# Laying the value stage's stationary operands 192 bytes, not 64, from its moving ones

## The chip, the cores and the metric

One core of a Trainium2 chip runs the whole kernel. The metric is the device time in microseconds, as the median of several executions. A profiled execution of the kernel before supplies the rows below; its engines are TensorE (PE for matmuls, PEld for its weight loads), VectorE (DVE), ScalarE (ACT), GpSimd (POOL) and SyncE (SP).

## The reference, cut to what matters

Eight sequences of 576 tokens with 8 heads of 64 go through attention inside chunks of 64 tokens, and its output through a channel mix. All is float32.

```python
scores = scale * q_c @ k_c^T                  # within each chunk of 64 tokens
attn = softmax(scores);  x = attn @ v_c       # x: (8, 576, 512)
x_prev = x moved down by one token
xk = mu_k * x + (1 - mu_k) * x_prev
xr = mu_r * x + (1 - mu_r) * x_prev
k = maximum(xk @ w_k, 0)                      # 512 -> 1024, "key stage"
v = (k * k) @ w_v                             # 1024 -> 512, "value stage"
out = sigmoid(xr @ w_r) * v                   # "receptance stage"
```

## The kernel before, in words

The 4608 tokens are cut into 18 groups of 256. For each group TensorE does, in an order written out by hand (the table `START` for groups 0 and 1 and the loading of the weights, the table `GROUP` for every later group): scores and softmax transposes of the next group, the key stage K (line 636), the receptance stage R (line 689) and the value stage (line 720 for groups 0 to 3, line 910 for groups 4 to 17). The order of every engine's instructions is fixed by these tables.

Each operand of K, R and the value stage is split into a high and a low part in a reduced 32-bit format, and a product takes three matmuls (high by high, high by low, low by high; `PASSES`).

- K: the stationary operand is a 128 by 128 block of the weight `wk`, the moving one 256 tokens of the mixed input `xk`. 18 groups of 96 matmuls.
- R: stationary is a block of the mixed input `xr`, moving are 512 columns of `wr`. 18 groups of 24 matmuls.
- Value stage: stationary is a block of the key stage's results (`kk`, or `ks`, sums of blocks of them), moving are 256 columns of a weight quarter (`b`). Groups 0 to 3 take 96 matmuls each; groups 4 to 17 use seven products of 12 matmuls instead of eight, 84 each.

Every matmul has its own weight load (PEld), which TensorE runs while the matmul before it streams its moving operand. So two reads of on-chip memory (SBUF) go on together: the moving operand of one matmul and the stationary operand of the next.

Where a tile lies in SBUF follows from the order in which `pool(...)` is called on lines 110 to 123: pools are placed one behind the other, and every buffer of a pool has the size of its largest tile. The first pool starts at 128 modulo 256, behind a few constants. Nearly all tiles are multiples of 256 bytes per partition, except, ahead of the stages' operands, three small tiles, each in a pool of its own: `mu2` (64 bytes, pool `par`), the row maxima `m` (64 bytes, pool `par_m`) and the row sums `z` (32 bytes and padding to 64, pool `par_z`). These three shift everything behind them by 64 bytes modulo 256. Bytes of the start addresses, modulo 256, in the built program:

| tiles | pool | before | after |
|---|---|---|---|
| `wr`, `xr` (R: moving, stationary) | rp | 128, 128 | 128, 128 |
| `kk`, `ks` (value stage: stationary), `rr`, weight staging | mx | 128 | 0 |
| `wk` (K: stationary), `b` quarters (value stage: moving) | wts, tmp | 192 | 192 |
| other value weights `b1` | mo | 192 | 192 |
| `xk` (K: moving) | kp | 0 | 0 |
| `mu2` / `m` / `z` | par / par_m / par_z | 128 / 192 / 0 | 192 / 128 / 0 |
| `qT`, `kT`, `p`, `v`, rings | ld, att | 64 | 64 |

Blocks inside these tiles start at multiples of 512 bytes (of 1024 for the weights), so the table holds for every block. "Moving minus stationary", modulo 256, is 64 in K before and after, 0 in R before and after, and in the value stage 64 before and 192 after.

Two short uses of TensorE in the loading stage also matter below: the first three token tiles are mixed by matmuls with diagonal matrices (line 580; 128 columns, plain float32, each instruction shown as two matmul records), stationary `diag` at 192, moving `x`, whose first buffer starts at 64 and whose second starts at 128 modulo 256.

Of the kernel before, what the change touches and what calls it, by code (L numbers as in the profile page):

```python
# [81 lines left out]
def tile_chunk_attention_channel_mix(  # L82
# [24 lines left out]
    def pool(name, bufs=1):  # L107
        return ctx.enter_context(tc.tile_pool(name=name, bufs=bufs))

    const = pool("const")  # L110
    rp = pool("rp")
    mx = pool("mx")
    par = pool("par")
    wts = pool("wts")
    tmp = pool("tmp", 2)
    par_m = pool("par_m")
    kp = pool("kp")
    par_z = pool("par_z")
    ld = pool("ld")
    att = pool("att", 2)  # L120
# [1191 lines left out]
```

## Time and profile before

| | us |
|---|---|
| median of 3 runs | 594.36 |
| the runs | 592.47 to 594.52 |
| the profiled execution | 592.36 |
| its span, first to last instruction | 590.6 |
| TensorE busy in it | 580.4 |
| VectorE busy | 459.2 |
| ScalarE busy | 354.4 |

A matmul's row shows its own latency (about 280 ns for 256 columns), but matmuls overlap: the next starts long before the one before it ends. What a stage costs is therefore the pitch, the time from one matmul's start to the next one's. In a chain or a timeline, a piece or the distance between two starts divided by the number of matmuls between them is the pitch.

### The profile page before, as it was taken

How to read it: one execution, taken by the hardware profiler on the slowest of the kernel's cores; microseconds unless marked ns; L12 is line 12 of the kernel's file. 1: busy time of each engine (PE TensorE's matmuls, PEld its weight loads, DVE VectorE, ACT ScalarE, POOL GpSimd, SP SyncE). 2: the span in 40 equal slices, each digit the busy share in tenths (PEclk: the TensorE clock that was granted, in tenths of full speed). 3: DMA queues.
4: the chain of work that ended last, by engine and by line, in shares of the span. 5: the costliest groups of instructions: out<-in, count | busy, mean ns of one | idle time of the engine just before them, and what ended most of it. 6: DMA issues, size and time to landing. Idle time of an engine off the chain costs nothing.

```text
span 590.6 us, 15313 instructions
## 1 busy us (share of the span) xinstructions
PE 580.4 (98%) x6497; PEld 549.0 (93%) x6497; DVE 459.2 (78%) x763; ACT 354.4 (60%) x530; POOL 0.7 (0%) x6
## 2 busy tenths in 40 slices
PE   8899999999999999999999999999999999999997
PEld 7779999999899999999999999999999999999997
DVE  2799898659698878887877696978797878876734
ACT  4898964535648483838292929292928383747461
POOL 0000000000000000000000000000000000000000
PEclk9999999999999999999999999999999999999999
DMA  9997422432434343434212434343434243010000
GB/s 283 219 319 172 102 52 74 95 76 51 75 76 74 76 72 80 72 84 71 60 23 64 69 87 66 82 71 85 65 86 72 75 66 82 9 50 25 2 37 37
DMA packets 183988, 49.25 MB, mean 83 GB/s; under 512 B 169576, under 2 KB 175728, under 8 KB 183920
## 3 DMA queue, kind: packets, MB, share of 16 engines
q1 hardware_dynamic: 183904, 48.27, 36.3%
q8 instruction: 51, 0.84, 0.6%
q14 instruction: 17, 0.14, 0.1%
q10 hardware_dynamic: 16, 0.00, 0.0%
HBM read 38.80 MB, written 9.44 MB: 82 GB/s over the span
## 4 chain that ended last, share of the span: by engine, by line
PE 90%; DVE 5%; DMA 2%; ACT 1%; SPq 1%; issue 0%; DVEq 0%; ACTq 0%
PE pk L636 33%; PE pr L689 17%; PE vx L910 13%; PE vyz L910 10%; PE pv L720 7%; PE xps L1092 3%; PE s L1018 3%; DMA wr_st<-in_moe_w_r 2%; PE pt L1074 2%; PE mxk L580 1%; PE mxr L580 1%; DVE bs L747 1%; SPq L186 1%; PE xps L494 0%; PE s L410 0%; DVE bs L766 0%
## 5 line engine op out<-in xcount | busy, mean ns | idle before, releaser
L636 PE MATMUL pk<-xkhi,wk 128*128 128x256 f32 x1152 | 208.2, 281 | 0.0
L636 PEld LDWEIGHTS pk<-xkhi,wk 128*128 128x128 f32 x1152 | 177.2, 187 | 1.2
L636 PE MATMUL pk<-xklo,wk 128*128 128x256 f32 x576 | 160.7, 279 | 0.0
L656 ACT ACTIVATE rr<-pk 128x512 f32<-128x512 f32 x56 | 33.0, 589 | 126.7 <-PE pk L636 126.6
L636 PEld LDWEIGHTS pk<-xklo,wk 128*128 128x128 f32 x576 | 108.3, 188 | 0.1
L689 PE MATMUL pr<-wr,xrhi 128*128 128x512 f32 x288 | 92.3, 401 | 0.0
L910 PE MATMUL vyz<-b,kk 128*128 128x256 f32 x504 | 66.1, 279 | 0.0
L910 PE MATMUL vx<-b,ks 128*128 128x256 f32 x504 | 66.1, 279 | 0.0
L910 PEld LDWEIGHTS vx<-b,ks 128*128 128x128 f32 x504 | 62.3, 188 | 0.0
L910 PEld LDWEIGHTS vyz<-b,kk 128*128 128x128 f32 x504 | 62.3, 188 | 0.0
L689 PEld LDWEIGHTS pr<-wr,xrhi 128*128 128x128 f32 x288 | 51.5, 188 | 10.4
L689 PE MATMUL pr<-wr,xrlo 128*128 128x512 f32 x144 | 56.4, 392 | 0.0
L720 PE MATMUL pv<-b,kk 128*128 128x256 f32 x384 | 46.4, 280 | 0.0
L720 PEld LDWEIGHTS pv<-b,kk 128*128 128x128 f32 x384 | 45.8, 188 | 0.2
L747 DVE TENSOR_TENSOR kk<-rr,kk 128x1024 fp32r<-128x1024 f32 x28 | 33.1, 1222 | 10.4 <-ACT kk L894 10.3
L663 ACT ACTIVATE rr<-rr 128x512 f32<-128x512 f32 x56 | 35.4, 633 | 1.8
L939 ACT ACTIVATE u<-vx 128x256 f32<-128x256 f32 x28 | 10.8, 385 | 42.1 <-PE vx L910 42.1
L689 PEld LDWEIGHTS pr<-wr,xrlo 128*128 128x128 f32 x144 | 27.0, 188 | 5.9
L856 DVE TENSOR_TENSOR ss<-rr 128x512 f32<-128x512 f32 x14 | 9.7, 693 | 27.3 <-ACT rr L663 27.3
L1154 DVE SCALAR_TENSOR_TENSOR mk<-d,mu,x 128x256 f32<-128x256 f32 (+3 forms) x80 | 27.7, 414 | 0.4
L1154 DVE SCALAR_TENSOR_TENSOR mr<-d,mu,x 128x256 f32<-128x256 f32 (+3 forms) x80 | 27.5, 412 | 0.0
L1047 DVE TENSOR_REDUCE z<-p 128x16 f32<-128x1024 f32 x15 | 18.2, 1214 | 11.3 <-ACT p L1043 11.3
(130 smaller groups left out, 885.8 us busy)
## 6 DMA issues: line engine op xcount, KB each, us to landing
v<-in_v SPq DMA_DIRECT2D x144, 64.0 KB, 2.4
out<-sg SPq DMA_DIRECT2D x36, 256.0 KB, 2.4
q_ring<-in_q SPq DMA_DIRECT2D x192, 36.0 KB, 2.0
k_ring<-in_k SPq DMA_DIRECT2D x192, 36.0 KB, 2.0
wk_st<-in_moe_w_k SPq DMA_DIRECT2D x4, 1024.0 KB, 12.0
wv_st<-in_moe_w_v SPq DMA_DIRECT2D x4, 1024.0 KB, 7.7
wr_st<-in_moe_w_r SPq DMA_DIRECT2D x2, 1024.0 KB, 10.3
q_ring<-in_q SPq DMA_DIRECT2D x2, 512.0 KB, 6.8
```

Of the source, the lines that this page charges most:

```text
L580: nc.tensor.matmul(m[:, cb, s : s + w], diag[nm, n][:, cb], x[:, cb, c0 : c0 + w], start=(n == 0), stop=(n == 1),)
L636: nc.tensor.matmul(pk[:, e, :], wk[a][:, cb, f * P : (f + 1) * P], xk[b][:, cb, :], start=(n == 0), stop=(n == 3 * NB - 1),)
L656: nc.scalar.activation(r, T[f"pk{g}{fp}"], AF.Relu)
L663: nc.scalar.activation(r, r, AF.Square)
L689: nc.tensor.matmul(pr, xr[a][:, cb, tl * TT : (tl + 1) * TT], wr[b][:, cb, :], start=(n == 0), stop=(n == 3 * NB - 1),)
L720: nc.tensor.matmul(T[f"pv{g}{tl}"][:, cols[c]], kk[a][:, f, tok[tl]], quarter(f // HF, c)[:, b, f % HF, :], start=(f == 0 and n == 0 and c ...
L747: nc.vector.tensor_tensor(to, x, y, ALU.subtract)
L910: nc.tensor.matmul(to, a[i][:, f, :], weight(w, j, f), start=first and f == 0 and n == 0, stop=f == HF - 1 and n == 2, skip_group_check=True,)
L1018: nc.tensor.matmul(T[f"s{g}"][halves[e], j, tl, hp, :], qT[halves[j], hp, cols], kT[halves[j], hp, cols], start=True, stop=True,)
L1047: nc.vector.tensor_reduce(out=T[f"z{g}"], in_=p(), axis=AX.X, op=ALU.add)
L1092: nc.tensor.matmul(T[f"xps{g}"][halves[c], 2 * j + a, tl * TT + e * CH : tl * TT + (e + 1) * CH], T[f"v{2 * g + tl}"][halves[j], hp, e, :] ...
L1154: nc.vector.scalar_tensor_tensor(out=to[:, cb, s : s + w], in0=T[f"d{g}"][:, cb, s : s + w], scalar=mu[:, cb : cb + 1], in1=T[f"xg{g}"][:, ...
```

## The change

Three pools change places; no instruction is added, removed or moved on any engine, and every tile keeps its size.

```diff
     const = pool("const")
     rp = pool("rp")
-    mx = pool("mx")
-    par = pool("par")
+    par_m = pool("par_m")
     wts = pool("wts")
     tmp = pool("tmp", 2)
-    par_m = pool("par_m")
+    par = pool("par")
     kp = pool("kp")
+    mx = pool("mx")
     par_z = pool("par_z")
```

The pool `mx`, which holds the key stage's results, is laid behind `kp`, which holds the mixed key input. `par` and `par_m`, both of 64 bytes, swap, so that the weights stay at 192 and the key input at 0.

## Rows read from the trace of the kernel before

**Rows 1.** The page: span, and busy time of each engine with its share.
```profile
span 590.6 us, 15313 instructions
PE 580.4 (98%) x6497; PEld 549.0 (93%) x6497; DVE 459.2 (78%) x763; ACT 354.4 (60%) x530; POOL 0.7 (0%) x6
```

**Rows 2.** The page: the chain that ended last, shares of the span by engine.
```profile
PE 90%; DVE 5%; DMA 2%; ACT 1%; SPq 1%; issue 0%; DVEq 0%; ACTq 0%
```

**Rows 3.** Waits of TensorE's matmuls, the longest three (us in total, times, longest).
```profile
PE s L410 <- DVE p L430: 1.5, 1, 1.5
PE mxk L580 <- DVE x L515: 1.4, 1, 1.4
PE s L410 <- ACT pT L143: 1.3, 1, 1.3
```

**Rows 4.** One group's period by stretch: busy us (x), clock, DMA share, GB/s.
```profile
199.18:229.33 30.15, 30.15 (x346) 28.61 (x340) 24.71 (x44) 17.90 (x27) 0.00 (x0) 1.00 0.38 76
```

**Rows 5.** Groups of instructions by line and shape: the value stage's matmuls.
```profile
L910 PE MATMUL vyz<-b,kk 128*128 128x256 f32 x504 | 66.1, 279 | 0.0
L910 PE MATMUL vx<-b,ks 128*128 128x256 f32 x504 | 66.1, 279 | 0.0
L720 PE MATMUL pv<-b,kk 128*128 128x256 f32 x384 | 46.4, 280 | 0.0
L910 PE MATMUL vx<-b,kk 128*128 128x256 f32 x168 | 22.1, 280 | 0.0
```

**Rows 6.** Timeline of TensorE, value stage of group 4: start, us, what.
```profile
188.10 1.58 PE L910 MATMUL vx<-b,kk 128*128 128x256 f32 x12
189.52 1.57 PE L910 MATMUL vyz<-b,kk 128*128 128x256 f32 x12
...
196.58 1.57 PE L910 MATMUL vx<-b,ks 128*128 128x256 f32 x12
```

**Rows 7.** The chain in order of time: K of group 1 (start, us).
```profile
67.71 8.48 PE pk L636 x72
```

**Rows 8.** Timeline of TensorE: K of group 0, pieces of one and two matmuls.
```profile
54.06 0.28 PE L636 MATMUL pk<-xklo,wk 128*128 128x256 f32 x1
...
54.40 0.28 PE L636 MATMUL pk<-xklo,wk 128*128 128x256 f32 x1
...
55.76 0.28 PE L636 MATMUL pk<-xklo,wk 128*128 128x256 f32 x1
...
62.11 0.61 PE L689 MATMUL pr<-wr,xrhi 128*128 128x512 f32 x2
```

**Rows 9.** The chain in order of time: R of group 1, behind that K.
```profile
62.27 5.44 PE pr L689 x24
```

**Rows 10.** Timeline of TensorE: R of the last group, behind a K at its usual pitch.
```profile
571.14 0.63 PE L689 MATMUL pr<-wr,xrhi 128*128 128x512 f32 x2
571.61 0.40 PE L689 MATMUL pr<-wr,xrlo 128*128 128x512 f32 x1
...
572.53 0.62 PE L689 MATMUL pr<-wr,xrhi 128*128 128x512 f32 x2
...
573.91 0.61 PE L689 MATMUL pr<-wr,xrhi 128*128 128x512 f32 x2
...
576.63 0.51 PE L910 MATMUL vx<-b,kk 128*128 128x256 f32 x3
```

**Rows 11.** Timeline of TensorE: mixing by diagonal matrices, token tiles 0 and 2.
```profile
26.14 2.05 PE L580 MATMUL mxk<-x,diag_k 128*128 128x128 f32 x16
51.23 2.05 PE L580 MATMUL mxk<-x,diag_k 128*128 128x128 f32 x16
```

**Rows 12.** Timeline of TensorE: first two matmuls of K in group 5, behind the scores.
```profile
199.18 0.38 PE L636 MATMUL pk<-xkhi,wk 128*128 128x256 f32 x1
199.40 0.28 PE L636 MATMUL pk<-xklo,wk 128*128 128x256 f32 x1
```

**Rows 13.** Groups of instructions: subtraction in the value stage's operands, VectorE.
```profile
L747 DVE TENSOR_TENSOR kk<-rr,kk 128x1024 fp32r<-128x1024 f32 x28 | 33.1, 1222 | 10.4 <-ACT kk L894 10.3
L672 DVE TENSOR_TENSOR kk<-relu,kk 128x512 fp32r<-128x512 f32 x16 | 10.8, 686 | 9.5 <-ACT kk L143 9.4
```

## The prediction

> **What bounds the kernel now.** Read the page's first and fourth part together. TensorE is busy for 580.4 of 590.6 us [rows 1] and carries 90% of the chain that ended last [rows 2]. The view of waits shows that its matmuls hardly wait: the three longest waits are 1.5, 1.4 and 1.3 us, once each, all in the loading stage [rows 3]. Then read one period by stretch: in the 30.15 us of a group TensorE is busy throughout, VectorE for 24.71 and ScalarE for 17.90, at a granted clock of 1.00, the 2.4 GHz level [rows 4]. So the time is the sum of TensorE's pitches, and a nanosecond on the pitch of a stage is paid once per matmul, with nothing to hide it; in the other direction a gain is kept, since VectorE has 5.4 us of room in each period and ScalarE 12.
>
> The value stage has 504 + 504 + 384 + 168 = 1560 matmuls [rows 5]. Their pitch: from 188.10 to 196.58 us there are six blocks of 12, so 8.48 us for 72, 117.8 ns [rows 6]. 1560 of these are 183.8 us, 31% of the span. One nanosecond more or less is 1.56 us.
>
> K has the same pitch, 8.48 us for 72 matmuls or 117.8 ns [rows 7], and the same 64 bytes between its operands. 256 columns at 2.4 GHz last 106.7 ns, so each matmul of both stages pays 11.1 ns beyond its columns. Not all of this is fixed. One stretch of K in group 0 runs faster with the same tiles: from 54.40 to 55.76 us it issues 12 matmuls, 113.3 ns each, and from 54.06 to 62.11 there are 71 in 8.05 us, still 113.4 [rows 8]. R behind it runs at 5.44 us for 24 or 226.7 ns [rows 9], exactly twice 113.3 for twice the columns. I call this the smooth pace. Behind a K at its usual pitch, R starts off it: its first six matmuls take 571.14 to 572.53 us, 231.7 ns each, the first two 0.47 us or 235 each; later twelve, from 573.91 to 576.63, are at 226.7 again [rows 10]. So R, with 0 bytes between its operands, falls back to the smooth pace by itself, and K and the value stage, at 64, mostly do not and pay 4.5 ns a matmul. The trace fits a collision of two reads (a moving operand and the next stationary one) that depends on when the two start, and perhaps on the distance of their addresses.
>
> **The change part by part.** No instruction moves, so every count, wait and queue stays. What is new are addresses.
>
> K, R, scores and transposes: the distance between their operands stays 64, 0 and so on. Cost 0. The smooth stretch of K may be lost or another one won: 71 matmuls by 4.5 ns, 0.3 us either way.
>
> The loading stage: weights staged in `mx` are converted elsewhere in memory, same instructions. Cost 0; TensorE waits there for a few us in all [rows 3], and a DMA is indifferent as far as any row tells.
>
> ScalarE and VectorE on `kk`, `rr`, `ks`: a subtraction of 1024 columns takes 1222 ns with both inputs in `mx`, one of 512 takes 686 ns with one input in `mx` and one 64 bytes further, in another pool [rows 13]. Per column that is 1.19 and 1.34 ns, the same once a fixed part of some 150 ns is taken off both. So distance does not show on VectorE; cost 0, and 5.4 us of room in a period hides what might come. If that cover were gone, 1 us in each of 14 periods would be 14 us.
>
> The value stage: the distance goes from 64 to 192, and its pitch is the whole question. No row shows three-pass matmuls of 256 columns at 192, so I bound it. From below by the smooth pace: 113.3 - 117.8 = -4.5 ns, by 1560, -7.0 us. From above by what R pays where it is off the smooth pace: 235 - 226.7 = 8.3 ns in one weight load's worth of stream; added to 113.3 this is 121.6, +3.8 ns, +5.9 us; the rows are rounded to 10 ns, so that the two could have been 240, which gives 126.6, +8.8 ns, +13.7 us. Further off lies a weight load that isn't hidden at all: behind the scores K's first matmul has a pitch of 220 ns [rows 12], which would be +102 ns and +159 us; I exclude it as nothing changes in what is issued ahead, and keep it out of the range. R's mean over six, 231.7 or 5.0 over the smooth pace, would give 118.3, as good as now.
>
> I take 121 ns, near R's dearest rows: +3.2 ns by 1560 is +5.0 us. The profiled execution goes from 592.36 to 597.4. The median of the runs lies 2.0 us above it (594.36), so the forecast is 599.4, in round terms 599. Why the dear side: at 64 the moving operand lies one 64-byte step ahead of the stationary one and runs away from it, since it covers 1024 bytes while the weight load covers 512; at 192 it lies one step behind and must pass it early, in a stream that has no columns in hand yet. K's observed stretch at 113.3 shows that at 64 passing can be free. This is an argument, not a row.
>
> The Trainium skill speaks against any change here. "SBUF — State Buffer", section "Who interferes with whom", gives TensorE two independent read ports, one for the moving operand and one for weight loads, and says that it waits for no one; "TensorE: Matmul & The Clock Gate", section "Back-to-back issue gap", puts the warm gap at columns over 2.4 plus 2.5 ns. By these pages the value stage would be at 109.2 ns at any distance and the change would cost nothing, 594.4; the trace has 117.8 there and 113.3 at best, so the figure does not hold here, while that addresses don't matter remains possible and is the first rival.
>
> **The rivals.** First, no change: the pitch does not care for the distance. For it: plain float32 mixing takes 2.05 us for 16 matmuls when `x` starts 128 bytes from `diag` modulo 256, and 2.05 again when it starts 192 from it [rows 11]; and K has two paces at one and the same distance [rows 7, 8], so timing alone can explain them. Also 192 is 64 on the other side, and a collision might be symmetric. Against it: those mixing matmuls pass 128 columns in about 112 ns, half the rate of the value stage, where a read that is late has time. Time: 594.4, the runs' own 592.5 to 594.5.
>
> Second, faster: at 192 the value stage falls into the smooth pace, as R does at 0 after six matmuls. For it: the pace exists at the same width, and the value stage always follows R, which by then is in it [rows 10]. Against it: K entered from a smooth R in group 1 at 67.71 us and did not stay smooth [rows 7, 9]. Price: -7.0 us, 587.4; with half of its matmuls smooth -3.5, 590.9.
>
> Third, the change does nothing of what it says because a matmul that needs the distance is fed from other tiles: excluded for all but the `b1` weights by the address table, and these lie at 192 as well. So it is given no chance.
>
> The forecast is itself the slower side. It decides from about 119.7 ns on (+1.9 ns, +3 us, the bound of 0.5%).
>
> **How the numbers follow.** Forecast, slower: 0.45. No change: 0.25. Faster: 0.30. A difference under 0.5% (3 us) cannot be told from none here, as three runs alone spread over 2 us. Within the slower case 597.5 to 605.5 is its own range, the top between 121.6 and 126.6 ns. The whole range goes from the smooth pace on a quick run, 587.4 less 1.4, 586, to 605.5. Both signs are real, so the range takes in all three cases, and only a slower pace than any nearby row is left out.
>
> **What would show it.** In the changed kernel's timeline, blocks of 12 value matmuls start every 1.41 us now; 1.45 would show the forecast, 1.36 the smooth pace, 1.41 no change. K must stay at 2.83 us per 24 and R at 2.72 to 2.77 per 12; if K moves too, the distance is not the cause. The engines' order and TensorE's waits should be as before. If the value pitch stands and the time moves, I am wrong on the loading stage or VectorE; if the pitch falls to 113.3, I am wrong on which side of the stationary operand is the better one.

## The result, and the profile after

The changed kernel took 588.29 us, median of 6 runs (586.07 to 588.54), against 593.48 for the kernel before, median of 6 on the same chip (592.42 to 594.52). The ratio is 0.9916 with a 95% interval of 0.99 to 0.9932: faster by 0.84%, some 5 us. The forecast was 599.0, slower. The profiled execution took 586.07 us against 592.36, 6.29 us less, and its span went from 590.6 to 584.3. The times of either kernel fall into two clusters some 2 us apart (before, three runs at 592.42 to 592.59 and three at 594.36 to 594.52; after, one at 586.07 with a mean granted clock of 1.000 and five at 588.22 to 588.54 with 0.997), so that the gain is some 6 us when like is put against like and 5 by the medians, which mix them; single times further down carry the same scatter.

The page, first and fourth part, of the kernel after (span; busy time, share and instructions of each engine; chain by engine):

```profile
span 584.3 us, 15313 instructions
PE 573.4 (98%) x6497; PEld 542.2 (93%) x6497; DVE 459.3 (79%) x763; ACT 354.2 (61%) x530; POOL 0.7 (0%) x6
...
PE 92%; DVE 5%; ACT 1%; DMA 1%; issue 0%; DVEq 0%; ACTq 0%
```

The counts are those of [rows 1], and VectorE and ScalarE are busy as long as before to within 0.2 us. TensorE alone is busy for 7.0 us less. Its longest three waits are the three of [rows 3], the same to the digit, so none of them went.

Groups of instructions by line and shape answer to [rows 5], but tell nothing of the pitch (the second number behind the bar is one matmul's latency); the subtraction of [rows 13] takes 1222 ns as before:

```profile
L910 PE MATMUL vyz<-b,kk 128*128 128x256 f32 x504 | 66.1, 281 | 0.0
L910 PE MATMUL vx<-b,ks 128*128 128x256 f32 x504 | 66.0, 281 | 0.0
L720 PE MATMUL pv<-b,kk 128*128 128x256 f32 x384 | 45.6, 279 | 0.0
```

The pitch is read from starts. The timeline of TensorE in the value stage of group 4 (start, us, what), against [rows 6]: blocks of 12 start 1.41 us apart, and six of them take 186.63 to 195.11, 8.48 us, 117.8 ns a matmul, just as before. In the last group they start 1.36 us apart from the second block on, 113.3 ns:

```profile
186.63 1.57 PE L910 MATMUL vx<-b,kk 128*128 128x256 f32 x12
188.04 1.58 PE L910 MATMUL vyz<-b,kk 128*128 128x256 f32 x12
...
195.11 1.58 PE L910 MATMUL vx<-b,ks 128*128 128x256 f32 x12
...
570.65 1.54 PE L910 MATMUL vx<-b,kk 128*128 128x256 f32 x12
572.03 1.52 PE L910 MATMUL vyz<-b,kk 128*128 128x256 f32 x12
573.39 1.52 PE L910 MATMUL vx<-b,ks 128*128 128x256 f32 x12
574.75 1.52 PE L910 MATMUL vyz<-b,kk 128*128 128x256 f32 x12
```

What did move is K, whose operands lie as far apart as they did. In the chain in order of time, the 96 matmuls of K are one piece per group. Two groups of the kernel before, then the same two after, with the stages that follow:

```profile
259.56 11.50 PE pk L636 x96
...
289.71 11.50 PE pk L636 x96
```

```profile
257.67 11.08 PE pk L636 x96
268.75 0.87 PE pt L1074 x8
269.62 2.75 PE pr L689 x12
272.38 1.09 PE xps L1092 x64
273.47 2.96 PE pr L689 x12
276.43 1.42 PE vx L910 x12
277.84 1.41 PE vyz L910 x12
...
287.41 11.08 PE pk L636 x96
```

0.42 us in each of 13 groups is 5.5 us. One period by stretch is 29.70 us where [rows 4] had 30.15, at the same granted clock of 1.00, 2.4 GHz:

```profile
227.50:257.20 29.70, 29.70 (x351) 28.15 (x345) 24.46 (x40) 17.84 (x26) 0.00 (x0) 1.00 0.39 77
```

Summed from the start times of all matmuls of a stage, within each group:

| Stage | before, us | after, us | groups at the smooth pace, after |
|---|---|---|---|
| K (distance 64 in both) | 202.60 | 197.18 | 3, 4, 6 to 16; group 0 in part, as before |
| value stage (64, then 192) | 181.61 | 180.53 | 0, 1, 17 |
| R (distance 0 in both) | 94.28 | 94.26 | |

K gave 5.4 us, the value stage 1.1, together 6.5 of a span shorter by 6.3. So the question was no longer what a distance of 192 costs, but why K ran faster at a distance that hadn't changed.

**Where in the beat K starts.** The paces point at it. 113.3 ns is 17 times 6.67 ns and R's 226.7 ns is 34 times 6.67 (16 cycles of 2.4 GHz). In the run of the kernel before, all settled stretches of R start at the same remainder modulo 6.67 ns, over 500 us, with a drift of 0.7 ns (up to 1.1 in the other runs). I call that R's beat, and give the start of another matmul as its lag in ns behind it. This is worked out from starts that the trace keeps in whole ns, so it is good to about 0.3 ns:

```
first matmul of K (the pitches from it on)     lag      pace
before, groups 2 to 16   222 117 118 117 118   5.3-6.3  117.8
after, groups 3, 4, 6-16 222 113 113 114 113   1.0-2.0  113.3
after, group 2           222 117 118 117 118   5.7      117.8
after, group 5           222 117 119 117 118   0.7      117.8
```

And the changed distance can move that start: it alters the few irregular pitches with which the value stage ahead of the scores begins. From the last matmul of R in group 11, ten pitches are 227 118 118 120 118 117 119 117 118 118 = 1290 ns before and 233 122 120 117 118 118 117 119 117 118 = 1299 after. 9 ns are one beat and 2.3 ns; K's lag moved from 5.8 on the mean to 1.6, forward by 2.5 modulo 6.67. That is a reading of two traces. The groups that missed fit it as well: group 2 of the kernel after starts where K was off the pace before, at 5.7. Two theories were put against each other: ENTRY (the instant at which K starts chooses its pace; the addresses matter only through it) and ADDRESS (the new places of the tiles make K faster by themselves).

### The profile page after: what moved, and what is told of

Same layout as the page of the kernel before. It is cut to its first block, busy times and chain, and to the rows that moved or that the text cites. A ratio compares the mean times of both kernels' runs of the same rounds, so it can differ in the third digit from the quotient of the medians.

```text
span 584.3 us, 15313 instructions
## 1 busy us (share of the span) xinstructions
PE 573.4 (98%) x6497; PEld 542.2 (93%) x6497; DVE 459.3 (79%) x763; ACT 354.2 (61%) x530; POOL 0.7 (0%) x6
## 4 chain that ended last, share of the span: by engine, by line
PE 92%; DVE 5%; ACT 1%; DMA 1%; issue 0%; DVEq 0%; ACTq 0%
PE pk L636 32%; PE pr L689 17%; PE vx L910 13%; PE vyz L910 10%; PE pv L720 7%; PE xps L1092 3%; PE s L1018 3%; PE pt L1074 2%; PE trq L367 1%; PE trk L367 1%; DMA q_ring<-in_q 1%; PE mxk L580 1%; PE s L410 1%; PE mxr L580 1%; DVE bs L747 1%; PE warm L1221 1%
## 5 line engine op out<-in xcount | busy, mean ns | idle before, releaser
L636 PE MATMUL pk<-xkhi,wk 128*128 128x256 f32 x1152 | 202.7, 278 | 0.0
L636 PEld LDWEIGHTS pk<-xkhi,wk 128*128 128x128 f32 x1152 | 175.4, 188 | 1.2
L747 DVE TENSOR_TENSOR kk<-rr,kk 128x1024 fp32r<-128x1024 f32 x28 | 33.1, 1222 | 10.4 <-ACT kk L894 10.3
L747 DVE TENSOR_TENSOR ks<-ss,ks 128x512 fp32r<-128x512 f32 x42 | 26.5, 686 | 0.0
```

The costliest lines, as they stand in the source:

```text
L636: nc.tensor.matmul(pk[:, e, :], wk[a][:, cb, f * P : (f + 1) * P], xk[b][:, cb, :], start=(n == 0), stop=(n == 3 * NB - 1),)
L747: nc.vector.tensor_tensor(to, x, y, ALU.subtract)
```

## The experiments

**K shifted, nothing moved.** The addresses are those of the kernel before. From group 2 on one more plain float32 matmul of 64 to 67 columns (64 in the diff below) stands right ahead of K's first one, writing where K then starts afresh:

```diff
+            if g >= 2 and fp == 0:
+                nc.tensor.matmul(
+                    pk[:, 0, :64], f32(wk[0][:, 0, :P]), f32(xk[0][:, 0, :64]), start=True, stop=True
+                )
```

> Addresses as before the change. Ahead of K's first matmul in groups 2 to 17 stands one extra plain float32 matmul of 64 columns into K's own accumulator, which K then overwrites. Its four versions (64, 65, 66, 67 columns) differ by one column, estimated at 1.7 ns from the 112 ns that a 128-column record of this kind takes (two records a matmul). Theory ENTRY: K's pace (113.3 or 117.8 ns) is set by the instant at which K is entered, on a beat of about 6.67 ns, and the change moved that instant; then of the four versions at least one has K at 113.3 ns in 10 or more of groups 2 to 16, and at least one has it at 117.8 in 10 or more, though no tile has moved. Theory ADDRESS: K runs at 113.3 because the results kk lie elsewhere (their writes by ScalarE and VectorE no longer meet K's reads); then K stays at 117.8 in groups 2 to 16 of all four versions. The extra matmul itself costs 0.1 to 0.25 us a group, 1.6 to 4 us in all, in every version.

> As e1_shift64 with 65 columns. ENTRY: K's pace in groups 2 to 16 differs from that in at least one of the other three versions by 4.5 ns a matmul, 0.42 us a group. ADDRESS: 117.8 ns here as in the others.

> As e1_shift64 with 66 columns. ENTRY: K's pace in groups 2 to 16 differs from that in at least one of the other three versions by 4.5 ns a matmul, 0.42 us a group. ADDRESS: 117.8 ns here as in the others.

> As e1_shift64 with 67 columns. ENTRY: K's pace in groups 2 to 16 differs from that in at least one of the other three versions by 4.5 ns a matmul, 0.42 us a group. ADDRESS: 117.8 ns here as in the others.

Measured, one run each, against 592.46: 596.55, 598.09, 595.91 and 595.84 us. K was at 117.8 in groups 2 to 17 of all four, so ENTRY's expectation was missed. The chain of the one with 64 columns:

```profile
261.75 0.36 PE pk L632 x2
262.12 11.37 PE pk L640 x96
```

But the edit doesn't only shift. K's first matmul no longer follows 64-column scores, and its pitch fell from 221 to 201 to 205 ns. Nor did the four lengths spread K's start: its lag was 2.8 to 3.8 ns in all four. Its second matmul came at 0.3 to 1.3 with 64 columns and at 4.5 to 5.5 with the other three; in the smooth groups of the changed kernel it comes at 3.2 on the mean. So none of the four hit that place, and the experiment tells neither theory from the other. In the run with 64 columns the value stage of group 17 went at 113.3 ns, with the old distance of 64: the smooth pace there doesn't need 192.

**The scores shifted instead.** The extra matmul now stands ahead of the scores, so K is still entered from the scores and only comes later, by one column (of a matmul shown as two records) from kernel to kernel. Addresses as before; the diff has 58 columns:

```diff
+            nc.tensor.matmul(T[f"s{g}"][:, 0, 0, 0, :58], ident, ident[:, :58], start=True, stop=True)
```

> Addresses as before the change. One extra plain float32 matmul of 57 columns (its result is overwritten) stands ahead of the scores of each group from group 3 on, behind the value stage and so one stage ahead of K, and K itself is entered as before, from the scores. Its four versions have 57, 58, 59 and 60 columns, so that K is entered at instants some 1.7 ns apart (estimated from 112 ns for a 128-column record, two records). Theory ENTRY, sharpened by the first four runs: the instant of K's first matmul, counted modulo 6.667 ns from the beat on which R settles in the same run, was 5.3 to 6.3 ns before the change (K at 117.8) and 1.0 to 2.0 behind it (K at 113.3; 117.8 where it was 0.7 or 5.7). So K is at 113.3 ns in every group whose entry falls at 1.0 to 2.0 and at 117.8 where it falls at 5.3 to 6.3, and of the four versions at least one has 113.3 in most of groups 4 to 16. Theory ADDRESS: 117.8 in groups 3 to 16 of all four. The extra matmul costs 0.1 to 0.3 us a group; a K at 113.3 gives back 0.42 us.

> As e2_delay57 with 58 columns: ENTRY expects K's entry 1.7 ns later on the beat than there, and K's pace by the phase it comes to; ADDRESS expects 117.8.

> As e2_delay57 with 59 columns: ENTRY expects K's entry 3.3 ns later on the beat than there, and K's pace by the phase it comes to; ADDRESS expects 117.8.

> As e2_delay57 with 60 columns: ENTRY expects K's entry 5.0 ns later on the beat than there, and K's pace by the phase it comes to; ADDRESS expects 117.8.

Measured, one run each, against 594.33: 596.28, 589.88, 596.38 and 596.60 us. The lags of K's first matmul, and its pace in groups 2 to 16:

```
columns   lag (mean)     K       time, us
57        0.3-1.3 (0.8)  117.8   596.28
58        1.3-2.2 (1.7)  113.3   589.88
59        2.0-3.0        117.8   596.38
60        3.0-3.7        117.8   596.60
```

Three chains over the same stretch, of 57, 58 and 59 columns; a group's K is 11.50 and 11.51 us in the outer ones and 11.08 between them:

```profile
262.17 11.50 PE pk L636 x96
...
292.47 11.50 PE pk L636 x96
```

```profile
259.79 11.08 PE pk L636 x96
270.87 0.87 PE pt L1075 x8
...
289.69 11.08 PE pk L636 x96
```

```profile
261.80 11.51 PE pk L636 x96
...
292.14 11.51 PE pk L636 x96
```

One column more, and the kernel gains 6.4 us; one more, and it is lost. No tile was moved. ADDRESS falls as the explanation of K: the gain is to be had without the change, and groups 2 and 5 of the changed kernel lack it with the tiles at their new places. The place that K must hit is some 1 ns wide, out of 6.67; group 5 of the changed kernel, with its lag of 0.7, misses it as the kernel with 57 columns does. A column moved the entry by 0.8 ns, half of what I expected.

**Other distances.** Only the order of the pools differs, so that the operands of the value stage (v) and of K lie at a given distance; no instruction moves. One product of seven, the fifth block of 12 in groups 4 to 17, takes the weights `b1` from another pool and stays at 64 in all four. As an example the one with both at 0 (`par` and `par_m` leave their places for ones behind `kp`; the others are of the same kind):

```diff
     rp = pool("rp")
     mx = pool("mx")
-    par = pool("par")
     wts = pool("wts")
     tmp = pool("tmp", 2)
-    par_m = pool("par_m")
     kp = pool("kp")
+    par = pool("par")
+    par_m = pool("par_m")
     par_z = pool("par_z")
```

> Only the order of the pools differs from the kernel before: value operands 0 bytes apart (64 in the products with the weights b1), key operands still 64. Theory ENTRY: distances have no price of their own, a stage runs at 113.3 or 117.8 ns by the instant at which it is entered; so the value stage's groups are each at one of the two, and K's groups too, in whatever mix the new instants give (total 586 to 594.5 us). Theory SELF-SETTLING: R settles on its smooth pace from any start because its operands are 0 bytes apart; then the value stage at 0 does so too, 113.3 ns in nearly all groups but for its first six matmuls of each and the b1 products, 6 us less than before at K's pace of before (587 to 589). Theory DISTANCE (the forecast's): 0 is another price for the value stage, over 117.8 or under 113.3.

> Value operands 128 bytes apart (64 in the products with b1 becomes 64 as moving b1 stays at 192 and ks at 128), key operands 64. ENTRY: each group's stage at 113.3 or 117.8, total 586 to 594.5 us. SELF-SETTLING says nothing here. DISTANCE: a third pace for the value stage.

> Value and key operands both 0 bytes apart. ENTRY: 113.3 or 117.8 in each group's stage by its instant of entry, total between 579 and 594.5. SELF-SETTLING: both stages at 113.3 in nearly all groups, 12 to 14 us less than before (579 to 582). DISTANCE: other paces.

> Key operands 192 bytes apart, value operands 64 as before. ENTRY: the value stage is entered from R as before and stays at 117.8, K is at 113.3 or 117.8 by its instant; total 587 to 594.5. DISTANCE: K shows a pace of its own at 192.

Measured, one run each, against 594.48, with the sums from the start times:

```
value  K     time, us   value stage                 K
0      64    591.61     184.57 us, 120.0            196.66 us, 113.3 in groups 2-16
128    64    595.97     183.79, 120.0, later 118.6  202.60, 117.8
0      0     600.52     184.57, 120.0               206.60 us, 120.0 everywhere
64     192   586.25     181.62, 117.8               196.21 us, 113.3 in groups 2-17, 0 in part
```

In the first three kernels the block with `b1` runs at 117.8 ns behind blocks at 120.0. Chains over the same stretch, of value 0 and K 0, of value 128 and K 64 (in both the block of 1.42 or 1.41 us is the one with `b1`), then of value 64 and K 192:

```profile
263.80 11.71 PE pk L636 x96
275.51 0.87 PE pt L1074 x8
...
286.05 1.44 PE vx L910 x12
287.49 1.44 PE vyz L910 x12
288.93 1.42 PE vx L910 x12
```

```profile
285.26 1.44 PE vyz L910 x12
286.70 1.41 PE vx L910 x12
288.12 1.43 PE vyz L910 x12
```

```profile
257.89 11.10 PE pk L636 x96
...
278.07 1.41 PE vyz L910 x12
...
287.64 11.10 PE pk L636 x96
```

That a distance of 0 settles to the smooth pace by itself, as R does, is refuted: with three-pass matmuls of 256 columns it settles at 120.0 ns, 18 times 6.67 and the dearest settled pace seen, and K at 0 has 11.71 us a group. So the distance has a price after all: 0 has 120.0; 128 has 120.0 as well (pitches of 117, 120 and 123 over and over) and, behind the block with `b1`, 118.6; 64 has 117.8 or 113.3. And for K 192 differs from 64 in how it catches: K at 192 begins off the pace in most groups and is in it after three to five matmuls (229 122 116 114 113 ns), where K at 64 is in it from its second matmul or, from group 2 on, not at all. In the kernel with K at 64 and the value stage at 0, K became smooth too, but from another place: it started 6.3 to 0.5 ns behind the beat, and at 0.3 to 1.3 (57 columns) it had been off the pace. Its two tiles lie 64 bytes lower there, at the same distance. So the place to hit is not the same wherever the tiles lie, and whether a new start or the new addresses made K smooth in that kernel is not shown.

**Timed, and both stages at 192.** The one column, K at 192, both at 192, and both at 192 with an extra matmul ahead of the value stage in groups 4 to 17 (to keep it from following R). The diff is that of the last one:

```diff
     const = pool("const")
     rp = pool("rp")
-    mx = pool("mx")
+    kp = pool("kp")
     par = pool("par")
     wts = pool("wts")
     tmp = pool("tmp", 2)
     par_m = pool("par_m")
-    kp = pool("kp")
+    mx = pool("mx")
     par_z = pool("par_z")
...
+            nc.tensor.matmul(X()[:, :64], ident, ident[:, :64], start=True, stop=True)
```

> The kernel of e2_delay58 again, timed: addresses as before the change, one extra 58-column matmul ahead of the scores. ENTRY: K at 113.3 ns in groups 2 to 16 again, 588.5 to 591 us, faster than the kernel before by 3.5 to 5 us though it does more work. If its single look was chance, 594 to 597.

> The kernel of e3_v64_k192 again, timed: key operands 192 bytes apart, value operands 64. If 192 draws K to the smooth pace from nearly any entry, K is at 113.3 from its fourth matmul on in all groups but group 1 again and the time 586 to 589, at or under the changed kernel's. If its entries only happened to fall well, times scatter up to 594.

> Both key and value operands 192 bytes apart. WIDE CATCH (at 192 a stage settles on the smooth pace from any entry except straight out of R): K at 113.3 in all groups but 1, the value stage at 113.3 in groups 0, 1 and 17, which are not entered from R or enter late on its beat, and at 117.8 in groups 2 to 16: 1 us less than e4_v64_k192_timed. DISTANCE (a price per distance): the value stage at one pace in all 18 groups.

> As e4_v192_k192 with one extra plain float32 matmul of 64 columns between R and the value stage in groups 4 to 17, overwritten by what follows, so that the value stage is no longer entered straight out of R. WIDE CATCH: the value stage at 113.3 in most of groups 4 to 17, a gain of 0.37 us a group, 14 groups 5.2 us, less the extra matmul's 0.1 to 0.3 us each: 1 to 4 us under e4_v192_k192. If R has nothing to do with it: 117.8 as there, and 1.4 to 4 us slower than it.

Measured on one chip, against 594.39 (median of 7, 592.38 to 594.52):

| Kernel | us (range) | ratio | 95% |
|---|---|---|---|
| 58 columns ahead of the scores | 589.62 (588.65-590.95) | 0.9923 | 0.9895-0.9951 |
| K at 192, value stage at 64 | 587.07 (586.16-588.55) | 0.9886 | 0.9861-0.991 |
| both at 192 | 587.5 (585.15-587.68) | 0.9881 | 0.9857-0.9906 |
| both at 192, 64 columns ahead of the value stage | 589.78 (589.35-590.45) | 0.993 | 0.9912-0.9948 |

The one column holds under repetition, as does K at 192. The second trace of the kernel with 58 columns has K as in the first, but not the value stage of group 4: that was smooth in the first, at 64, and at 117.8 in the second. So one program can take either pace from execution to execution. With both at 192 the value stage was smooth in groups 0, 1 and 4 and at 117.8 in the others (17 was expected among the smooth, and 4 wasn't); its sum is 180.55 us, 1.1 less than at 64, which the times of the second and third kernel can't tell. These two repeat what the change did to K's start: with K at 192 in both, its lag in groups 6 to 16 was 5.3 to 6.3 with the value stage at 64 and 1.3 to 1.8 with it at 192. The extra matmul did not do what was expected: the value stage behind it was smooth in 0, 1 and 4 only. Chains of the third and the fourth; in both the blocks of 12 take 1.41:

```profile
259.07 11.10 PE pk L636 x96
...
279.26 1.41 PE vyz L910 x12
```

```profile
277.68 0.17 PE vx L922 x2
277.85 1.47 PE vx L910 x12
279.32 1.41 PE vyz L910 x12
```

So leaving R isn't enough, just as for K in the first experiment: where one lands counts.

**Another length of the same gap.** The last kernel with 61 and with 68 columns in place of 64.

> As e4_v192_k192_gap, with 61 columns in the extra matmul instead of 64. ENTRY: in that kernel the value stage was at 113.3 ns only in group 4, entered 3.3 ns behind R's beat, and at 117.8 in groups 5 to 17, entered at 5.3 to 6.3. Other lengths of the extra matmul move the entry; groups entered at 3.3 to 4.0 are at 113.3, those at 5.3 to 6.3 stay at 117.8. If the new entries fall at 3.3 to 4.0, 13 groups gain 0.37 us each, 4.8 us, and the kernel takes 584 to 586; if not, 589 to 591. If the value stage at 192 cannot be settled by entry in these groups, 117.8 at every entry.

> As e5_gap61 with 68 columns: the same reading of entry and pace; 584 to 586 us if its entries fall at 3.3 to 4.0 ns behind R's beat, 589 to 591 if not.

Against 593.8 (median of 7): 61 columns 584.07 us (583.95 to 585.55), ratio 0.9841 (0.9823 to 0.986); 68 columns 589.94 (588.09 to 590.39), ratio 0.9926 (0.9901 to 0.9951). With 61 the value stage was smooth in groups 0, 1 and 4 to 17 and its sum 177.02 us; with 68 in 0, 1, 4 and 17. The chain of 61, then of 68:

```profile
256.65 11.10 PE pk L636 x96
...
275.42 0.17 PE vx L922 x2
275.58 1.43 PE vx L910 x12
277.01 1.36 PE vyz L910 x12
278.37 1.36 PE vx L910 x12
...
286.26 11.10 PE pk L636 x96
```

```profile
278.37 0.17 PE vx L922 x2
278.54 1.46 PE vx L910 x12
280.00 1.41 PE vyz L910 x12
281.42 1.41 PE vx L910 x12
```

With 61 columns the blocks of 12 start 1.36 us apart, which is K's smooth pace, and this is the fastest kernel of the study: 1.6% below the kernel before, where the changed one is 0.84% below it. (The two were timed on different chips; by their ratios 0.75% lies between them.) It does an added matmul in each of groups 4 to 17 for it.

Its time lies in the expected range, but not for the reason given there: it was expected from a start 3.3 to 4.0 ns behind the beat, and 117.8 from 5.3 to 6.3, but the value stage's first matmul came at 5.3 to 6.3 with 61 columns as with 64. So it was luck that this length worked. What differs is the first pitch, 206 and 202 ns, so that the second matmul is at about 5.0 and at 1.7. That does not settle it either: with 68 columns group 4 was smooth with its second matmul at 1.7. Perhaps two instants count, that of the matmul and that of the next weight load; no run here varies one without the other. K at 192 missed once here: with 61 columns its group 17 ran at 117.8.

## Why the prediction was wrong, point by point

**What bounds the kernel** held. TensorE's pitches are the time: 6.5 us less on them is 6.3 us less of span, with the three longest waits as they were and VectorE and ScalarE unchanged. That the room in each period would keep a gain held too.

Two steps failed. By the profiled execution the forecast was 597.4 us and 586.07 were measured, 11.3 less. K, which stood at 0, gave 5.4 us; the value stage, which stood at +5.0, gave 1.1, so that it came out 6.1 under its term.

**K, R, scores: cost 0, a smooth stretch lost or won, 0.3 us either way.** This step failed on what decided the result; for R it held (94.28 and 94.26 us). The smooth stretch of K was in the text, with its cause half named ("depends on when the two start"), and then sized as if only the 71 matmuls of group 0 could change. The bound should have been all of K: 18 groups of 95 pitches by 4.5 ns are 7.7 us. It measured -5.4 us, for 13 groups. The step also took each stage's addresses as its own affair. K's start follows from the end of the value stage, through the scores, and K has two paces at one distance, chosen by that start; so an edit in one stage can move the time in another in which nothing changed.

**The value stage, 121 ns, +5.0 us.** Wrong in sign. In 15 of 18 groups it stayed at 117.8, what the first rival said, and in 3 it fell to 113.3, what the second said: -1.1 us. No group at 192 settled above 117.8. The argument that the moving operand "must pass it early" at 192 was drawn from geometry, not from a row, and the runs speak against its direction: K at 192 was smooth in every group from 2 to 17 of five traces and in all but one of a sixth, while K at 64 was off the pace in all these groups in nine of thirteen traces. The upper bound drawn from R's irregular pitches, 121.6 and more, was never reached by a whole stage; the dearest settled pace that any distance showed is 120.0, at 0 and at 128.

**The rival of no change** said that addresses don't matter. That is refuted by 0 and 128 (600.52 us with both stages at 0; 120.0 ns beside 117.8 within one stage), though 64 and 192 do share their two paces, as its remark that 192 is 64 on the other side allowed.

**The rival of faster** gave 587.4 by all 1560 value matmuls, 590.9 by half. The time came out near it, 588.29, by luck, for another reason: K. Its step that the value stage follows R, "which by then is in it", does not carry either; behind R at 192 it stayed off the pace in 15 groups.

**VectorE, ScalarE and loading at 0** held: 1222 ns for the subtraction as before, the three longest waits the same.

The range (586 to 605.5) held the time, though its lower part was meant for a smooth value stage, which did not come. The text's own test, "if K moves too, the distance is not the cause", pointed away from a price of the distance: K moved, the value stage mostly didn't. The new distance still acted, through K's start.

Shown by a run: K's pace follows from the instant of its start, at fixed addresses (57, 58, 59 columns); the paces that were seen differ with the distance (0, 64, 128, 192). Read from traces only, in two pairs of kernels: that the value stage at 192 moves K's start, by its first pitches. Open: why K at 64 misses in group 17, where no scores stand ahead of it, at a lag of 1.3 (kernel after) and 2.0 (58 columns); why its place differs in the kernel with the value stage at 0; what keeps the value stage at 192 off the pace in groups 2 and 3, where the kernel with 61 columns has no added matmul; what the 6.67 ns beat is in the chip. That two reads of SBUF collide was the prediction's picture; no run measured it, nor which of them would wait.

## What to carry to other kernels

Where matmuls run back to back, find out how many paces one stage has at the same tiles, and bound a change of addresses or of order by the gap between them times all matmuls of all such stages, not only those it touches. Before giving credit to a change of layout, undo it and shift the start by a column or two: here one column of an added matmul moved the time by 1.1% with no tile moved. To keep a pace, prefer a distance that falls into it from many starts over one that must be hit to the nanosecond. K at 192 did so in five kernels, in all of groups 2 to 17 but one, from lags of 1.3 to 1.8, 4.5 to 5.3 and 5.3 to 6.3; the value stage at 192, behind R, did not.

## What the runs showed of the hardware

- In products of three matmuls, those of 256 columns settled at a few paces, which differ with the distance of the two operands' starts modulo 256 bytes: 120.0 ns at 0, 120.0 or 118.6 at 128, 117.8 or 113.3 at 64 and 192. In one stage whose other blocks were at 0 or 128 and ran at 120.0, the block at 64 ran at 117.8.
- A pace once taken was kept, as a rule, over a group's 95 pitches. At 64, with K's tiles where the kernel before has them modulo 256, K was smooth behind the scores where it started 1.0 to 2.2 ns of 6.67 behind R's beat, and not at 0.3 to 1.3 or at 2.0 to 3.0 (the edges overlap, as a lag is good to about 0.3); with both tiles 64 bytes lower it was smooth at 6.3 to 0.5.
- The same distance serves one width and not another: R, at 0 with 512 columns, runs at 226.7, twice the smooth pace; K at 0 with 256 columns at 120.0.
- The periods shown of the kernels before and after are at a granted clock of 1.00, 2.4 GHz, and the longest waits of TensorE don't tell of it: the three longest are the same in both. It is seen in the distance of starts, and it separates 600.52 us (both stages at 0, one run) from 584.07 (both at 192, 61 columns ahead).
